# Two MoE stages behind a linear attention: the K^T V units placed in the first 32 steps, and the loads ahead of step 0 reordered

## The chip, the cores and the metric

One core of a Trainium2 chip runs the whole program. The metric is the device time of one execution in microseconds (us), the median of three runs. The profile and its trace come from one further execution.

## The reference

```
# q, k, v: (8, 8, 576, 64) float32; g_norm: (64)
kv  = einsum('bhsd,bhse->bhde', k, v)            # per batch and head, 64 x 64
out = einsum('bhsd,bhde->bhse', q, kv)
rms = sqrt(mean(out * out, axis=-1) + 1e-6)
x   = (out / rms * g_norm)                       # -> (4608, 512)
h   = x @ w_in                                   # (512, 2048)
g   = (a0 + a1 h + a2 h^2 + a3 h^3) / (1 + |b0||h| + |b1|h^2 + 1e-6)
x   = g @ w_out                                  # (2048, 512)
out = ((x @ w1) * (x @ w2)) @ w3 @ w_out2        # (512,1024), (512,1024), (1024,1024), (1024,512)
```

The weights reach the kernel as 64-bit floats.

## The kernel before, in words

**Prelude.** The order of work ahead of the first step is written out by hand as a string of letters. K loads the next K^T V unit, Q the next tile of 128 rows of q, W the next raw weight tile (512 KB), C converts a raw weight tile, F finishes pending conversions, c loads the constants and d works on them, k does a unit's matmuls (`kv_part`, `kv_out`), and t, o, r, n, x are the stages of a q tile: transpose, product with K^T V, root mean square, normalisation with a second transpose, and evacuation to the high and low parts `xh` and `xl`. All loads go through SP's one queue, in program order.

**Units.** K^T V of one batch is five units: four of 128 rows by 512 values of K and of V (256 KB each), and a short one of 64 rows (128 KB each). There are 8 batches and so 40 units, u = 0 to 39. A unit's 16 half-width matmuls on 64 columns add into the single PSUM tile `kv`; after the fifth unit of a batch `kv_out` copies the sum out, for batches 0 and 1 into `kvbd`, for later ones through a tile `kve` to memory (`kvd`), from which `kv_load` fetches it when its q tiles come up. K and V of a unit have two buffers each, `kt` and `vt`.

**Conversion.** A raw weight tile is made into float32 by one operation on ACT and three on DVE (L149, L151, L155, L159), and split into a high part on ACT (L84) and a low part on DVE (L85). A pending list holds back the split by up to two tiles. `wa0` to `wa15` are the 128-column slices of `w_in`, `wb0` to `wb15` the 128-row slices of `w_out`. There are 32 tiles; 11 are converted in the prelude and the others in steps 0 to 21, as many a step as the digits of `CONV` say.

**Steps.** 192 steps g follow, each one slice m of the hidden dimension for one block j of 384 rows. `l1(g)` is 12 matmuls into one of two PSUM tiles `h` (L88 to L90); ACT, POOL and DVE work on `h` in `ew1`, `ewy`, `ew2`, `ew3` (L536 to L573); `l2(g - 3)` is 12 matmuls into four tiles `acc` (L500 to L503). Within a step the string `MIX` sets the order in which pieces of these and of the conversions are issued. The first blocks go through the slices as block 0 with m = 0 to 7, block 1 with m = 0 to 15, block 0 with m = 8 to 15, and then block after block.

**What is hung onto the steps.** `todo` has, for a step and a place in it, further functions. Place 4 is the end of the step, behind `l2`, and place 0 its start. Units 8 to 39 are at the ends of steps 0, 1, 3, 5, ... 61, one a step; behind unit u's matmuls stands the load of unit u + 2, which waits until they have read the buffers. SP's queue is in order, so loads issued later wait behind that load. q tiles from 4 on have their stages in the steps too.

**After the steps** come the two later products, in 48 and 19 slots and a part between them; the change doesn't touch them.

Of the kernel before, what the change touches and what calls it, by code (L numbers as in the profile page):

```python
# [8 lines left out]
F32 = mybir.dt.float32  # L9
# [9 lines left out]
def linear_attention_two_moe_kernel(  # L19
# [25 lines left out]
    B, H, S, D = q.shape  # L45
# [3 lines left out]
    P = 128  # L49
    KD = DM // P  # L50
    NP = H // 2
    MF = DFF // P
# [12 lines left out]
    wp = ctx.enter_context(tc.tile_pool(name="wp", bufs=1))  # L65
# [28 lines left out]
    wa, wb = {}, {}  # L94
    bits = [t.bitcast(I32) for t in (w_in, w_out, w1, w2, w3, w_out2)]
    w_in_b, w_out_b, w1_b, w2_b, w3_b, w_out2_b = bits
    W = 512
# [39 lines left out]
    def mix(order, **gens):  # L137

        for c in order:
            next(gens[c], None)  # L140
        for gen in gens.values():
            run(gen)
# [79 lines left out]
    atp = atp_cm.__enter__()  # L222
# [3 lines left out]
    def segs(i):  # L226

        r, left = [], P
        t = i * P
        while left:  # L230
            b, s = divmod(t, S)
            n = min(left, S - s)
            r.append((P - left, n, b, s))
            t += n
            left -= n
        return r

    kt, vt, qt = {}, {}, {}

    def load_tok(i, src, d, tag):  # L240
        t = atp.tile([P, H, D], F32, tag=tag, name=tag, bufs=2)
        for r0, n, b, s in segs(i):
            nc.sync.dma_start(out=t[r0:r0 + n], in_=src[b, :, s:s + n, :].rearrange("h s d -> s h d"))
        d[i] = t

    MT = S // P
    NU = B * (NP + 1)
    HG = H // NP

    def load_kv(u):  # L250

        b, r = divmod(u, NP + 1)
        for src, d, tag in ((k, kt, "kt"), (v, vt, "vt")) if u < NU else ():
            t = atp.tile([P, H * D], F32, tag=tag, name=tag, bufs=2)
            if r < NP:
                nc.sync.dma_start(
                    out=t.rearrange("p (h f) -> p h f", h=HG),
                    in_=src[b, r * HG:(r + 1) * HG, 0:MT * P, :].rearrange("h (p t) d -> p h (t d)", t=MT),
                )
            else:  # L260
                nc.sync.dma_start(
                    out=t[0:S - MT * P].rearrange("p (h d) -> p h d", h=H),
                    in_=src[b, :, MT * P:, :].rearrange("h s d -> s h d"),
                )
            d[u] = t

    def load_q(i):
        if i < NTILE:
            load_tok(i, q, qt, "qt")
# [147 lines left out]
    with tc.manual_schedule():  # L417
# [36 lines left out]
        def k_next(u):  # L454
            kv_part(u)
            kv_out(u)

        tile_ops = {
            "K": (load_kv,), "Q": (load_q,), "k": (k_next,), "t": (q_pe, q_out), "o": (o_pe, n_sq),
            "r": (n_rms, n_rsq), "n": (n_out, x_pe), "x": (x_out,),  # L460
        }
        whole = {"W": w_load, "C": w_conv, "F": conv_flush, "c": consts, "d": const_ops}
        nc.vector.memset(unit, 1.0)
        nc.scalar.activation(out=unit, in_=unit, func=AF.Abs_reciprocal_sqrt)
        for op in "KQKWKcKdkQkCtWCWkCWCFkKWkWCCWCWQWtCQoCtoKWtKWKrrooWWKQknrrKnnxxkWnxWCQkCxW":
            if op in whole:
                whole[op]()
            else:
                i = count.get(op, 0)
                count[op] = i + 1  # L470
                for f in tile_ops[op]:
                    f(i)
# [105 lines left out]


        KV0 = 8  # L580
        KV_STEPS = [0, 1] + list(range(3, 4 * MF, 2))
        todo = {}

        def at_step(g, place, f, i):
            todo.setdefault((g, place), []).append((f, i))

        def do(g, place):
            for f, i in todo.get((g, place), ()):
                f(i)
# [3 lines left out]

        AT_G = [0, 5, 10]
        AT_W = [4, 7, 7, 10, 12, 13, 16, 18, 28, 30]
        for g, u in zip(KV_STEPS, range(KV0, NU)):
            at_step(g, 4, kv_part, u)
            at_step(g, 4, load_kv, u + 2)
            at_step(g + 1, 0, kv_out, u)
        at_step(2 * MF - 1, 4, kv_load, 2)  # L600
        for i in range(T0, NTILE):
            j, t = divmod(i, TPB)
            if j < 3:
                g = (-2 if j == 1 else 3 * HM - 3) + 3 * t
                when = ((q_pe, 0, 4), (q_next, 0, 4), (q_out, 1, 0), (o_pe, 1, 1), (n_sq, 1, 2), (n_rms, 1, 3),
                        (n_rsq, 1, 4), (n_out, 2, 0), (x_pe, 2, 4), (x_out, 3, 0))
            else:
                g = (j - 1) * MF + AT_G[t]
# [9 lines left out]
        for s in range(2 * KF2):  # L618
            src, c = (w1_b, w2_b)[s % 2].rearrange("(k p) f -> p k f", p=P), s // 2
# [490 lines left out]
                prod_d(f["a"], n, A12, B21, False, late)  # L1110
            e_load(n + 3)

        MIX = "nntltsuysltsttunuuu", "snsnalttaltyasnt", "ntsnnltlsyttst"
        CONV = "21011011120111111111110"
        NG = NBA * MF
        LB = NG - MF
# [117 lines left out]
        def u_some(n):  # L1234
            for i in range(n):
                if not next(chain, False):
                    break
                yield
# [19 lines left out]
        for j in range(NPR):  # L1258
# [8 lines left out]
            if j:  # L1267
                for c in range(5):
                    n = 5 * (j - 1) + c
# [19 lines left out]
        for g in range(NG + SK):  # L1289
# [28 lines left out]
            if LB < g:  # L1318
                gens["t"] = u_some(int(PREP[g - LB]))
            mix("".join(x for x in MIX[(g >= len(CONV)) + (g > LB)] if x in gens), **gens)  # L1320
            do(g, 2)
# [67 lines left out]
```

## Time and profile before

| | |
|---|---|
| median of three runs | 1559.38 us (1557.82 to 1559.94) |
| the profiled execution's own time | 1558.43 us |
| its span, from the first instruction to the last | 1556.7 us |
| TensorE matmul (PE) busy | 1515.8 us, 97% of the span |
| VectorE (DVE) busy | 1243.2 us, 80% |
| ScalarE (ACT) busy | 1056.5 us, 68% |
| GpSimd (POOL) busy | 225.0 us, 14% |
| share of PE in the chain that ended last | 85% |

The span is what the trace covers; 1.7 us of the execution's time lie around it. A busy share is a mean over stretches that differ: it tells where an engine is full only when it is read stretch by stretch. Step 0 begins at 47.12 us, step 8 at 94.55, step 21 at 161.53, step 32 at 218.61, step 48 at 298.43, step 64 at 377.68, step 80 at 450.43, step 96 at 523.18 and step 112 at 596.75: the stretches below are cut there.

### The profile page before, as it was taken

The numbers are of one execution on the slowest core, as the hardware profiler recorded it, in microseconds if no ns is written. First come the engines' busy times: TensorE is split into PE (matmuls) and PEld (weight loads), VectorE is DVE, ScalarE is ACT, GpSimd is POOL, SyncE is SP. The second block draws the span as 40 slices with busy tenths as digits, with TensorE's granted clock in tenths as the row PEclk, the third lists the DMA queues.
The fourth block names the chain that finished last, engine by engine and source line by source line (L and its number), as shares of the span: only waits on it lengthen the run. The fifth ranks groups of instructions, "written<-read, shape, count | busy, mean of one in ns | idle before, by whom it ended". The sixth has DMA issues, their size and how long they took to land.

```text
span 1556.7 us, 26099 instructions
## 1 busy us (share of the span) xinstructions
PE 1515.8 (97%) x9640; PEld 1477.4 (95%) x9640; DVE 1243.2 (80%) x2374; ACT 1056.5 (68%) x2109; POOL 225.0 (14%) x201
## 2 busy tenths in 40 slices
PE   4899999999999999999999999999999999999999
PEld 3788999999999999999999999999999999899999
DVE  5899968777889888988888889877677675688875
ACT  4688877787888888888888888544344343555554
POOL 0122221222222222222222221000000000000000
PEclk9799999999999999999999999999999999999999
DMA  9644243231112111110101021443543534434452
GB/s 281 194 141 140 72 112 99 82 96 45 48 38 69 42 45 42 45 55 28 58 28 56 6 69 37 146 146 112 190 141 117 190 119 164 140 110 154 155 160 89
DMA packets 153456, 157.95 MB, mean 101 GB/s; under 512 B 57328, under 2 KB 131312, under 8 KB 153328
## 3 DMA queue, kind: packets, MB, share of 16 engines
q1 hardware_dynamic: 153328, 156.28, 32.0%
q8 instruction: 76, 1.25, 0.3%
q14 instruction: 52, 0.43, 0.1%
HBM read 106.43 MB, written 49.81 MB: 100 GB/s over the span
## 4 chain that ended last, share of the span: by engine, by line
PE 85%; DVE 9%; ACT 3%; DMA 1%; issue 1%; POOL 1%; SPq 0%; DVEq 0%; POOLq 0%
PE acc L787 11%; PE h L88 8%; PE h L90 8%; PE h L89 8%; PE acc L500 7%; PE acc L501 7%; PE acc L503 7%; PE acc L1045 5%; PE h L787 5%; PE at L787 3%; PE kv L787 3%; PE h L1045 2%; PE kv L1045 2%; PE at L1045 2%; PE at L360 1%
## 5 line engine op out<-in xcount | busy, mean ns | idle before, releaser
L550 POOL TENSOR_TENSOR s<-z,a 128x384 f32<-128x384 f32 x192 | 223.3, 1163 | 732.6 <-ACT z L547 663.4
L553 DVE TENSOR_TENSOR n<-n,h 128x384 f32<-128x384 f32 x192 | 105.5, 550 | 91.9 <-ACT n L548 89.9
L546 ACT ACTIVATE a<-h 128x384 f32<-128x384 f32 x192 | 94.2, 491 | 98.3 <-PE h L90 97.6
L571 DVE SCALAR_TENSOR_TENSOR n<-n,na,y 128x384 f32<-128x384 f32 x192 | 155.4, 809 | 0.0
L562 ACT ACTIVATE y<-s,epsq 128x384 f32<-128x384 f32 x192 | 118.2, 616 | 44.7 <-POOL s L550 43.6
L547 ACT ACTIVATE z<-a,ab 128x384 f32<-128x384 f32 x192 | 136.2, 709 | 6.4
L548 ACT ACTIVATE n<-h,na 128x384 f32<-128x384 f32 x192 | 125.8, 655 | 0.0
L555 DVE SCALAR_TENSOR_TENSOR n<-n,na,h 128x384 f32<-128x384 f32 x192 | 116.4, 606 | 0.5
L569 DVE SCALAR_TENSOR_TENSOR s<-s,y 128x384 f32<-128x384 f32 x192 | 109.3, 569 | 0.0
L538 DVE TENSOR_TENSOR lo<-n,hi 128x384 fp32r<-128x384 f32 x192 | 106.9, 557 | 0.0
L573 DVE SCALAR_TENSOR_TENSOR n<-s,n 128x384 f32<-128x384 f32 x192 | 105.5, 550 | 0.2
L563 ACT ACTIVATE y<-y 128x384 f32<-128x384 f32 x192 | 101.0, 526 | 6.1
L536 ACT CAST hi<-n 128x384 fp32r<-128x384 f32 x192 | 96.1, 500 | 1.1 <-DVE n L573 1.1
L286 PEld LDWEIGHTS kv<-vt,kt 128*64 128x64 f32 (+1 forms) x640 | 24.7, 151 | 25.7 <-DMA kt<-in_k_dram 17.0
L286 PE MATMUL kv<-vt,kt 128*64 128x64 f32 (+1 forms) x640 | 30.4, 243 | 16.2 <-DMA vt<-in_v_dram 16.2
L829 ACT COPY p<-kv 128x384 f32<-128x384 f32 x24 | 11.5, 480 | 38.5 <-PE kv L787 26.9
L829 ACT COPY p<-acc 128x384 f32<-128x384 f32 x24 | 11.5, 480 | 38.5 <-PE acc L787 30.9
L844 ACT COPY u<-acc 128x384 f32<-128x384 f32 x24 | 11.5, 480 | 31.6 <-PE acc L787 31.6
L360 PE MATMUL at<-kvbd,qT 128*128 128x128 f32 (+1 forms) x216 | 29.2, 285 | 3.1 <-DVE kvbd L303 2.7
L360 PEld LDWEIGHTS at<-kvbd,qT 128*128 128x128 f32 (+1 forms) x216 | 26.6, 184 | 5.2 <-POOL s L550 3.0
L844 ACT COPY u<-h 128x384 f32<-128x384 f32 x24 | 11.5, 480 | 28.1 <-PE h L787 26.9
L379 DVE TENSOR_REDUCE ms<-sq 128x8 f32<-128x512 f32 x36 | 24.4, 683 | 5.9 <-ACT sq L373 5.9
(1440 smaller groups left out, 4923.0 us busy)
## 6 DMA issues: line engine op xcount, KB each, us to landing
ed<-eo SPq DMA_DIRECT2D x48, 384.0 KB, 2.6
er<-ed SPq DMA_DIRECT2D x35, 512.0 KB, 3.8
x2d<-xev SPq DMA_DIRECT2D x48, 192.0 KB, 2.0
xr<-x2d SPq DMA_DIRECT2D x48, 192.0 KB, 3.9
out_dram<-o SPq DMA_DIRECT2D x36, 256.0 KB, 2.0
kt<-in_k_dram SPq DMA_DIRECT2D x32, 256.0 KB, 2.8
vt<-in_v_dram SPq DMA_DIRECT2D x32, 256.0 KB, 3.2
qt<-in_q_dram SPq DMA_DIRECT2D x32, 256.0 KB, 3.1
```

The lines of the kernel that those rows point to most:

```text
L88: nc.tensor.matmul(outp, lhsT=lh, rhs=rh, start=first, stop=False)
L89: nc.tensor.matmul(outp, lhsT=lh, rhs=rl, start=False, stop=False)
L90: nc.tensor.matmul(outp, lhsT=ll, rhs=rh, start=False, stop=last)
L547: nc.scalar.activation(out=z, in_=a, func=AF.Identity, scale=ab[:, 1:2], bias=ab[:, 0:1])
L548: nc.scalar.activation(out=n, in_=h, func=AF.Identity, scale=na[:, 3:4], bias=na[:, 2:3])
L550: nc.gpsimd.tensor_tensor(out=s, in0=z, in1=a, op=ALU.mult)
L555: nc.vector.scalar_tensor_tensor(out=n, in0=n, scalar=na[:, 1:2], in1=h, op0=ALU.add, op1=ALU.mult)
L562: nc.scalar.activation(out=y, in_=e["s"], func=AF.Abs_reciprocal_sqrt, bias=epsq[:, 0:1])
L569: nc.vector.scalar_tensor_tensor(out=s, in0=s, scalar=EPS_Q, in1=y, op0=ALU.add, op1=ALU.mult)
L571: nc.vector.scalar_tensor_tensor(out=n, in0=n, scalar=na[:, 0:1], in1=y, op0=ALU.add, op1=ALU.mult)
L787: nc.tensor.matmul(bank, lhsT=lh[:, sl], rhs=x, start=first and kk == 0 and n == 0, stop=kk == 1 and n == 2, skip_group_check=True,)
L1045: nc.tensor.matmul(bank, lhsT=l[:, c, :], rhs=r, start=first and c == 0 and x == 0, stop=c == KH - 1 and x == 2, skip_group_check=True,)
```

## The change

The prelude's string is a new permutation of the same letters, with the same number of each. Units 0 to 9 are loaded into places of weight tiles that are needed late (`wb15` to `wb8`, `wa15`, `wa14`), K and V as the two halves of one place named `near`; q tiles 0 to 3 go two by two into `wa13` and `wa12`. So the first ten units have a place of their own each, and `kt` and `vt` begin with unit 10. `KVC` gives the number of units at the end of each of the steps 0 to 33; its 32 units end at step 30. Where two units stand at the end of one step, the first one's `kv_out` follows it at once. `MIX` has a new order in the steps with conversions (0 to 22).

```diff
+    late = [f"wb{i}" for i in range(MF - 1, MF // 2 - 1, -1)] + [f"wa{i}" for i in range(MF - 1, MF // 2 - 1, -1)]
+    NEAR = 2 * (NP + 1)
+
+    def in_slot(n):
+        return wp.tile([P, 2, W], F32, tag=late[n], name="near")
+
+    qnear = {}
+
     def load_tok(i, src, d, tag):
-        t = atp.tile([P, H, D], F32, tag=tag, name=tag, bufs=2)
+        if i < 4:
+            if i % 2 == 0:
+                qnear[i // 2] = in_slot(NEAR + i // 2)
+            t = qnear[i // 2][:, i % 2, :].rearrange("p (h d) -> p h d", h=H)
+        else:
+            t = atp.tile([P, H, D], F32, tag=tag, name=tag, bufs=2)
...
         b, r = divmod(u, NP + 1)
-        for src, d, tag in ((k, kt, "kt"), (v, vt, "vt")) if u < NU else ():
-            t = atp.tile([P, H * D], F32, tag=tag, name=tag, bufs=2)
+        if u < NEAR:
+            near = in_slot(u)
+        for n, (src, d, tag) in enumerate(((k, kt, "kt"), (v, vt, "vt")) if u < NU else ()):
+            t = near[:, n, :] if u < NEAR else atp.tile([P, H * D], F32, tag=tag, name=tag, bufs=2)
...
-        for op in "KQKWKcKdkQkCtWCWkCWCFkKWkWCCWCWQWtCQoCtoKWtKWKrrooWWKQknrrKnnxxkWnxWCQkCxW":
+        for op in "KKWCkWWCWFCCQcKKKWWtCCWQkWkQdWQkkCtKWCoKtCWooKtKrWrWoQKrknWWnrWnnxxxQCkCkx":
...
-        KV_STEPS = [0, 1] + list(range(3, 4 * MF, 2))
+        KVC = "1101012122011121212111110102101000"
+        KV_STEPS = [g for g, n in enumerate(KVC) for _ in range(int(n))]
...
-        for g, u in zip(KV_STEPS, range(KV0, NU)):
+        for n, (g, u) in enumerate(zip(KV_STEPS, range(KV0, NU))):
             at_step(g, 4, kv_part, u)
             at_step(g, 4, load_kv, u + 2)
-            at_step(g + 1, 0, kv_out, u)
+            at_step(*((g, 4) if KV_STEPS[n + 1:n + 2] == [g] else (g + 1, 0)), kv_out, u)
...
-        MIX = "nntltsuysltsttunuuu", "snsnalttaltyasnt", "ntsnnltlsyttst"
+        MIX = "nntlsutlsutstunuytu", "snsnalttaltyasnt", "ntsnnltlsyttst"
```

**At the start of SP's queue** the loads of units, q tiles, weights and constants stand in this order before:

```order
L256 DMA kt<-in_k_dram 128x2x256
L256 DMA vt<-in_v_dram 128x2x256
L243 DMA qt<-in_q_dram 128x8x64
L256 DMA kt<-in_k_dram 128x2x256
L256 DMA vt<-in_v_dram 128x2x256
L104 DMA wa0r<-in_moe_w_in_dram 128x4x256
L256 DMA kt<-in_k_dram 128x2x256
L256 DMA vt<-in_v_dram 128x2x256
L206 DMA co_a<-in_moe_a_dram 128x4
```

and in this order now:

```order
L271 DMA near<-in_k_dram 128x2x256
L271 DMA near<-in_v_dram 128x2x256
L271 DMA near<-in_k_dram 128x2x256
L271 DMA near<-in_v_dram 128x2x256
L104 DMA wa0r<-in_moe_w_in_dram 128x4x256
L104 DMA wa1r<-in_moe_w_in_dram 128x4x256
L104 DMA wa2r<-in_moe_w_in_dram 128x4x256
L104 DMA wa3r<-in_moe_w_in_dram 128x4x256
L256 DMA near<-in_q_dram 128x8x64
```

Four weight tiles moved ahead of the first q tile, of units 2 to 4 and of the constants; the next weight tile, `wb0r`, follows behind those in both orders.

**Ahead of step 0 on PE** stand the last units of the prelude and the transposes of the four normalised tiles `xt`, before:

```order
L286 MATMUL kv_363<-vt_305,kt_303 64x64 x8
L403 MATMUL acc1_376<-ident_75,xt_374 128x128 x4
L403 MATMUL acc2_401<-ident_75,xt_399 128x128 x4
L403 MATMUL acc3_410<-ident_75,xt_408 128x128 x4
L286 MATMUL kv_363<-vt_318,kt_316 64x64 x8
L403 MATMUL at_435<-ident_75,xt_433 128x128 x4
L286 MATMUL kv_363<-vt_324,kt_322 64x64 x8
L88 MATMUL h_482<-xh_415,wa0hl_186 128x384
```

and now:

```order
L301 MATMUL kv_361<-near_259 64x64 x8
L418 MATMUL acc1_374<-ident_75,xt_372 128x128 x4
L418 MATMUL acc2_387<-ident_75,xt_385 128x128 x4
L418 MATMUL acc3_404<-ident_75,xt_402 128x128 x4
L418 MATMUL at_413<-ident_75,xt_411 128x128 x4
L301 MATMUL kv_361<-near_279 64x64 x8
L301 MATMUL kv_361<-near_313 64x64 x8
L88 MATMUL h_470<-xh_418,wa0hl_132 128x384
```

One unit moved from ahead of the fourth transpose to behind it, so two units stand between that transpose and step 0.

**At the end of step 8 on PE**, between the last matmuls of `l2(5)` and the first of `l1(9)`, stands nothing before:

```order
L503 MATMUL acc0_697<-lo_960,wb5hl_772 128x384
L503 MATMUL acc1_698<-lo_960,wb5hl_772 128x384
L503 MATMUL acc2_699<-lo_960,wb5hl_772 128x384
L503 MATMUL acc3_700<-lo_960,wb5hl_772 128x384
L88 MATMUL h_1055<-xh_470,wa1hl_196 128x384
```

and now two units (15 and 16):

```order
L518 MATMUL acc0_685<-lo_972,wb5hl_757 128x384
L518 MATMUL acc1_686<-lo_972,wb5hl_757 128x384
L518 MATMUL acc2_687<-lo_972,wb5hl_757 128x384
L518 MATMUL acc3_688<-lo_972,wb5hl_757 128x384
L301 MATMUL kv_1070<-vt_936,kt_934 64x64 x8
L301 MATMUL kv_1070<-vt_1010,kt_1008 64x64 x8
L88 MATMUL h_1095<-xh_460,wa1hl_135 128x384
```

Counted over the whole program: steps 0 to 7 had 5 units and have 7 (one more at step 6, which had none and has two), steps 8 to 20 had 6 and have 17, steps 21 to 31 had 6 and have 8, steps 32 to 61 had 15 and have none.

## Rows read from the trace of the kernel before

**Rows 1.** Busy time by stretch: steps 0-7, 8-20, 21-31, 32-47, 48-63, 64-79, 96-111.
```profile
core 0: us, PE busy (x) PEld busy (x) DVE busy (x) ACT busy (x) POOL busy (x), PEclk, DMA share, GB/s
...
47.12:94.55 47.43, 42.23 (x279) 39.03 (x277) 40.73 (x80) 34.83 (x68) 9.55 (x8) 0.86 0.59 174
94.55:161.53 66.98, 62.14 (x409) 57.16 (x409) 66.95 (x132) 58.75 (x111) 20.28 (x14) 1.00 0.46 140
161.53:218.61 57.08, 56.81 (x408) 54.15 (x408) 49.10 (x95) 46.95 (x93) 13.17 (x12) 1.00 0.27 75
218.61:298.43 79.82, 79.54 (x564) 76.14 (x561) 61.23 (x125) 60.30 (x117) 16.61 (x16) 1.00 0.35 103
298.43:377.68 79.25, 79.25 (x556) 76.11 (x553) 60.51 (x123) 61.28 (x120) 16.47 (x17) 1.00 0.28 79
377.68:450.43 72.75, 72.75 (x434) 72.16 (x434) 63.78 (x124) 60.94 (x120) 18.25 (x17) 1.00 0.16 46
523.18:596.75 73.57, 73.57 (x442) 72.56 (x442) 63.79 (x124) 61.07 (x120) 18.28 (x17) 1.00 0.16 46
```

**Rows 2.** Timeline of PE (start, us): first matmuls of steps 44, 45 and 46.
```profile
279.57 0.42 PE L88 MATMUL h<-xh,wa12hl 128*128 128x384 f32 x1
...
283.86 0.34 PE L88 MATMUL h<-xh,wa13hl 128*128 128x384 f32 x1
...
288.77 0.44 PE L88 MATMUL h<-xh,wa14hl 128*128 128x384 f32 x1
```

**Rows 3.** The same, steps 17 and 18 (in brackets: idle before, and its releaser).
```profile
141.25 0.45 PE L88 MATMUL h<-xh,wa9hl 128*128 128x384 f32 x1 [0.60 <-DVE n L555]
...
146.32 0.44 PE L88 MATMUL h<-xh,wa10hl 128*128 128x384 f32 x1
```

**Rows 4.** PE's waits in steps 8 to 20: us in total, times, longest.
```profile
PE h L88 <- DVE n L555: 4.3, 7, 0.9
```

**Rows 5.** Timeline of DVE in the prelude: conversions, then the normalisation.
```profile
11.62 0.42 DVE L151 TENSOR_SCALAR wa0r<-wa0r 128x512 int32<-128x512 uint32 x1
...
25.37 0.43 DVE L151 TENSOR_SCALAR wb0r<-wb0r 128x512 int32<-128x512 uint32 x1
...
36.50 1.27 DVE L379 TENSOR_REDUCE ms<-sq 128x8 f32<-128x512 f32 x2
...
44.21 0.69 DVE L396 TENSOR_TENSOR xt<-acc,ny 128x512 f32<-128x512 f32 x1
```

**Rows 6.** Timeline of SP: the issue of the load of `wb0r`.
```profile
15.52 1.21 SPq L104 DMA_DIRECT2D wb0r<-in_moe_w_out_dram  x1
```

**Rows 7.** That load among the DMA issues: size, us from issue to landing.
```profile
wb0r<-in_moe_w_out_dram SPq DMA_DIRECT2D x1, 512.0 KB, 7.2
```

**Rows 8.** Timeline of PE: last transpose and unit of the prelude, step 0.
```profile
45.05 1.09 PE L403 MATMUL at<-ident,xt 128*128 128x128 f32 x4 [0.53 <-DVE xt L396]
46.06 1.12 PE L286 MATMUL kv<-vt,kt 128*64 128x64 f32 x16
47.12 0.69 PE L88 MATMUL h<-xh,wa0hl 128*128 128x384 f32 x1
...
50.07 0.34 PE L88 MATMUL h<-xh,wa0hl 128*128 128x384 f32 x1
```

**Rows 9.** Busy time by stretch, as rows 1: the prelude, and around step 0.
```profile
11.60:47.12 35.52, 17.99 (x151) 15.08 (x147) 30.15 (x58) 20.40 (x41) 0.00 (x0) 0.90 0.90 275
...
40.00:50.00 10.00, 8.20 (x53) 6.91 (x54) 9.18 (x21) 5.32 (x11) 0.00 (x0) 0.50 0.57 163
```

**Rows 10.** Timeline of SP: a unit's loads behind the unit of step 13.
```profile
126.08 0.38 SPq L256 DMA_DIRECT2D kt<-in_k_dram  x1
126.50 0.47 SPq L256 DMA_DIRECT2D vt<-in_v_dram  x1
```

**Rows 11.** The second of them among the DMA issues, as rows 7.
```profile
vt<-in_v_dram SPq DMA_DIRECT2D x1, 256.0 KB, 3.0
```

**Rows 12.** Timeline of PE: the wait of step 2.
```profile
64.70 1.94 PE L360 MATMUL at<-kvbd,qT 128*64 128x128 f32 x8 [2.75 <-DVE kvbd L303]
```

## The prediction

> **What bounds the kernel now.** The table has PE busy for 97% of the span, so I looked for stretches where a unit's matmuls cost nothing. Busy time by stretch [rows 1] shows three kinds. From step 32 on PE is full: 79.54 of 79.82 us, then 79.25 of 79.25, while DVE is busy for about 61. In steps 8 to 20 it is DVE that is full, 66.95 of 66.98 us, and PE has 66.98 - 62.14 = 4.84 us idle. In steps 0 to 7 PE has 47.43 - 42.23 = 5.2 us idle and DVE 6.7; they wait for each other. The waits [rows 4] name what PE waits for in steps 8 to 20: 4.3 us in 7 waits for DVE's L555, the last reader of a tile `h`. The timeline shows it in the small: step 18 has no unit, and step 17, which has one, begins after 0.60 us of idle time that follow step 16, which has none; yet step 17 takes 146.32 - 141.25 = 5.07 us [rows 3]. A unit is there paid out of idle time. Where PE is full it is not: step 44 without a unit takes 283.86 - 279.57 = 4.29 us and step 45 with one 288.77 - 283.86 = 4.91 [rows 2].
>
> Ahead of step 0 the engines are far from full: PE 17.99 of 35.52 us, DVE 30.15, and the DMA engines at 0.90 and 275 GB/s [rows 9]. DVE begins its first conversion at 11.62 and `wb0`'s at 25.37, and at 36.50 turns to the normalisation of the first four q tiles, which ends in step 0 at 47.12 [rows 5, 8].
>
> **The change part by part.**
>
> *Steps 32 to 63 lose 15 units.* The same 16 slices without units are there in the same trace: steps 64 to 79 in 72.75 us, and steps 96 to 111, which like 48 to 63 hold one q tile that spans two batches, in 73.57 [rows 1]. So steps 32 to 47 come down from 79.82 to 72.75 (7.07 us, 8 units) and steps 48 to 63 from 79.25 to 73.57 (5.68 us, 7 units): **-12.75 us**, or 0.85 a unit. The direct price of 0.62 [rows 2] would give 15 x 0.62 = 9.3; that is the small end. I take 12.75, since it compares whole stretches with the q stages in them.
>
> *Steps 21 to 31 gain 2 units.* PE is full but for 57.08 - 56.81 = 0.27 us [rows 1]. Two units at 0.62 to 0.88 are 1.2 to 1.8, less the idle time: **+1.3** (1.0 to 1.8).
>
> *Steps 8 to 20 gain 11 units,* 11 x 0.62 = 6.8 us of PE work, into 4.84 us of idle time. PE busy 62.14 + 6.8 = 68.96, against 66.98: **+2.0**. The small end is 0: DVE's own 66.95 us are a floor, and PE's, at 4.29 a step and 0.62 a unit, is 13 x 4.29 + 17 x 0.62 = 66.3. The large end is 6.8, if no idle time can be used. I take the sum of busy times, since PE needs 5.5 us in a step with two units and 4.9 in one with one, DVE 5.07 in either, and the two sorts alternate.
>
> *Steps 0 to 7 gain 2 units,* both at step 6, where PE has no idle time ahead of it worth counting; the 5.2 us lie mainly in the waits of steps 1 and 2, the longest of them 2.75 us for the copy of `kvbd` [rows 12]. **+1.3** (0 to 1.8). The new `MIX` keeps the same operations on DVE in a step, and where DVE is full their order doesn't change their sum: nothing. If a reordered operation came to wait, it would show as idle time of DVE, which has none in steps 8 to 20.
>
> *The prelude.* `wb0r`, issued at 15.52, landed 7.2 us later, at 22.7 [rows 6, 7]. Up to and with it 5.25 MiB are loaded before and 5.0 now, for one q tile went behind it: 256 KB at 275 GB/s is 0.95 us. SP also no longer waits, ahead of these loads, for the first units to leave `kt` and `vt`; that can be worth up to the missing tenth of the DMA engines' time, some 1 us. So `wb0r` lands at about 21.0. DVE, which has then been through `wa0` to `wa3`, begins `wb0` 25.37 - 21.0 = 4.4 us sooner. But low parts of two weights and the copy of `kvbd`, three operations of about 0.65 us (two reductions take 1.27 [rows 5]), and the small ones on the constants stand behind that place now and ahead of it before: 2.0 us. The normalisation begins 2.4 us sooner. Of its end: before, the fourth `xt` runs at 44.21, and its transpose and one unit at 45.05 and 46.06 bring step 0 to 47.12 [rows 5, 8]. Now two of the evacuations to `xl` (about 0.69 each) come behind that `xt` instead of ahead of it, -1.4, and a second unit stands on PE behind the transpose, +1.06. Step 0 comes 2.4 + 0.3 = **2.7 us sooner**. The ends are 0 (the loads of units 2 to 4, the q tile and the constants ahead of `wb0r` eat it up) and 4.7 (the held-back operations find room). The places borrowed from late weights cost nothing: their units and q tiles are through before those weights are loaded.
>
> Sum: -12.75 + 1.3 + 2.0 + 1.3 - 2.7 = -10.85 us. The profiled execution took 1558.43, so 1547.6; the median lies 0.95 above it: **1548.5 us**.
>
> **The rivals.**
>
> *The loads come late (slower).* Before, a unit's loads had three steps or more. Now 12 units (13, 14, 16, 17, 18, 23, 24, 26, 27, 29, 30, 38) are loaded behind the unit two ahead of them, and are needed one step later, after 4.29 + 0.62 = 4.9 us. The loads behind the unit of step 13 show what it takes in a quiet queue: K issued at 126.08, V at 126.50, V landed after 3.0 more, 3.4 in all [rows 10, 11]; 1.5 us to spare. Against that: in steps 6 to 9 the loads of units 14 to 20, five weight tiles and a q tile are 6.0 MB in some 20 us, 296 GB/s, as much as the DMA engines moved in the prelude at 0.90, and there a load took 7.2 us [rows 7, 9]. PE would stand at each such unit, with `l1` and `l2` of the next step behind it. The gain is gone when the 12 wait 10.85 / 12 = 0.9 us each, that is when V lands 5.8 us behind the unit; at 7.7 it is 12 x 2.8 = 33 us, 1582 us. For most steps the weights are 4 tiles ahead and the queue is near empty, which speaks for 3.4 to 4.5.
>
> *The idle time can't be used.* PE and DVE hand over twice a step with only two tiles `h`; after a double step PE is 0.5 us late, DVE might then wait, and the next step gives nothing back. Steps 8 to 20 then pay 6.8 and steps 0 to 7 1.8: 1548.5 + 4.8 + 0.5 = 1553.8. For it: DVE has no idle time to lend. Against: step 17 above.
>
> *The change moves cost and saves none.* If the 15 units cost in the first 32 steps the 0.85 that they cost later, only the start is left: 1559.38 - 2.7 = 1556.7.
>
> *Step 0 is no earlier:* 1551.2. For it: eleven loads, four of them small, now lie between those of `wa3r` and `wb0r`, and two before.
>
> *The clock.* From 40 to 50 us the granted clock was 0.50, that is 1.2 GHz, after a stretch in which PE worked for half of the time [rows 9]; nine matmuls of step 0 took 50.07 - 47.12 = 2.95 us [rows 8], against 9 x 4.29 / 24 = 1.61 at 2.4 GHz [rows 2]. A shorter prelude with the same matmuls in it might bring the higher clock to step 0 and one of steps 2 and 3: -2.7, 1545.8. The Trainium skill (TensorE: Matmul & The Clock Gate, Part 1: The HAM clock gate) says that the clock is held down by default and that activity releases it; by that rule a prelude with fewer gaps would run step 0 faster. The trace agrees that it was low after a sparse stretch; what it will be here no row shows, and the sum leaves it as it is.
>
> **How the numbers follow.** The forecast, with its terms moving within their bounds (1545.5 to 1551.5): 0.55. Step 0 no earlier, 1551.2: 0.13. Idle time not usable, 1553.8: 0.12. The clock, 1545.8: 0.10. No saving, 1556.7: 0.05. Loads late: 0.05, of which a fifth ends near the old time. The range 1543.5 to 1554 holds the first four nearly whole, somewhat over 8 in 10. A difference of 0.2% is 3.1 us, about what a measurement can tell. Faster by more: 0.55 + 0.13 + 0.12 + 0.10 = 0.90. Within: 0.05 + 0.01 = 0.06. Slower: 0.04.
>
> **What would show it.** Right: steps 32 to 63 in 146 to 147 us instead of 159.1, with no unit in them; PE's idle time in steps 8 to 20 near zero, DVE's a little above it, the stretch 67 to 70 us; step 0 at 44 to 45 us and DVE at `wb0` near 21. Wrong: in steps 7 to 20, waits of the unit's matmuls for the loads of K or V (none now); idle time of PE ahead of L88 left at 4 us with the stretch at 72 or more; step 0 still at 47; a granted clock of 0.50 in more than the stretch around steps 0 to 3.

## The result, and the profile after

The changed kernel takes 1546.27 us (median of 4, 1545.43 to 1547.06), the kernel before on the same chip 1558.92 (1557.82 to 1559.94): a ratio of 0.9919, 95% interval 0.9902 to 0.9936, 12.65 us faster. The profiled execution took 1547.06 us with a span of 1545.3, 11.4 less than before.

Busy time by stretch of the changed kernel, which answers to [rows 1]: steps 0-7, 8-20, 21-31, 32-47, 48-63, 64-79, with the same columns.

```profile
45.32:91.21 45.89, 41.07 (x310) 37.55 (x308) 42.17 (x83) 35.79 (x70) 9.28 (x8) 0.93 0.53 170
91.21:161.30 70.09, 67.77 (x588) 63.01 (x585) 66.80 (x131) 58.36 (x113) 16.31 (x13) 1.00 0.71 218
161.30:218.95 57.65, 57.65 (x444) 55.33 (x441) 46.80 (x93) 46.65 (x93) 11.61 (x11) 1.00 0.33 93
218.95:292.34 73.39, 73.10 (x434) 72.18 (x433) 63.98 (x125) 59.42 (x115) 17.33 (x17) 1.00 0.18 53
292.34:365.89 73.55, 73.55 (x441) 72.57 (x441) 63.80 (x124) 61.01 (x120) 18.24 (x17) 1.00 0.16 46
365.89:438.63 72.74, 72.74 (x433) 72.18 (x433) 63.80 (x124) 60.94 (x120) 18.25 (x17) 1.00 0.16 46
```

Steps 32 to 63 now read like 64 to 79. Against [rows 1], in us:

| term | forecast | measured |
|---|---|---|
| step 0 begins (47.12 to 45.32) | -2.7 | -1.80 |
| steps 0-7 | +1.3 | -1.54 |
| steps 8-20 | +2.0 | +3.11 |
| steps 21-31 | +1.3 | +0.57 |
| steps 32-63 | -12.75 | -12.13 |
| after step 63 | 0 | +0.4 |
| sum | -10.85 | -11.4 |

PE's waits in steps 0 to 31 of the changed kernel (us in total, times, longest), to be held against [rows 4, 12]:

```profile
PE h L88 <- DVE n L570: 2.3, 1, 2.3
PE at L375 <- DVE kvbd L318: 2.1, 1, 2.1
PE kv L301 <- DMA vt<-in_v_dram: 1.7, 2, 1.2
PE acc L515 <- ACT xev L540: 0.6, 1, 0.6
PE at L362 <- DVE xl L427: 0.2, 1, 0.2
PE at L375 <- ACT qT L367: 0.2, 1, 0.2
```

The many short waits for DVE's last reader of `h` (L555 before, L570 now) have gone from steps 8 to 20; the one left is in steps 0 to 2. The third row is new: two units waited for the load of V. The fourth is a wait for `xev`, the copy that ACT makes of a finished tile `acc`. The timeline of PE shows the longer wait for V, at the end of step 9 (units 15 and 16, then 17, then 18; between them `l1(9)` and `l2(6)`), and last the other, of unit 24 at the end of step 15:

```profile
95.61 1.43 PE L301 MATMUL kv<-vt,kt 128*64 128x64 f32 x32
96.97 0.44 PE L88 MATMUL h<-xh,wa1hl 128*128 128x384 f32 x1
...
101.37 0.69 PE L301 MATMUL kv<-vt,kt 128*64 128x64 f32 x16
103.22 0.69 PE L301 MATMUL kv<-vt,kt 128*64 128x64 f32 x16 [1.16 <-DMA vt<-in_v_dram]
103.84 0.44 PE L88 MATMUL h<-xh,wa2hl 128*128 128x384 f32 x1
...
150.68 0.68 PE L301 MATMUL kv<-vt,kt 64*64 64x64 f32 x16 [0.50 <-DMA vt<-in_v_dram]
```

SP issues the loads of units 17 and 18 behind units 15 and 16, and the last of the four took 5.2 us where [rows 11] had 3.0; first the timeline of SP, then that load among the DMA issues (size, us to landing):

```profile
96.34 0.38 SPq L271 DMA_DIRECT2D kt<-in_k_dram  x1
96.76 0.47 SPq L271 DMA_DIRECT2D vt<-in_v_dram  x1
97.33 0.41 SPq L271 DMA_DIRECT2D kt<-in_k_dram  x1
97.84 0.41 SPq L271 DMA_DIRECT2D vt<-in_v_dram  x1
```

```profile
vt<-in_v_dram SPq DMA_DIRECT2D x1, 256.0 KB, 5.2
```

V of unit 18 so landed at about 103.0, 6.1 us behind the end of unit 16.

**The prelude.** Timeline of DVE, which answers to [rows 5]:

```profile
22.33 0.43 DVE L151 TENSOR_SCALAR wb0r<-wb0r 128x512 int32<-128x512 uint32 x1 [5.01 <-DMA wb0r<-in_moe_w_out_dram]
...
35.58 1.86 DVE L394 TENSOR_REDUCE ms<-sq 128x8 f32<-128x512 f32 x3
...
41.62 0.69 DVE L411 TENSOR_TENSOR xt<-acc,ny 128x512 f32<-128x512 f32 x1
```

The load it waits for, as [rows 6, 7], on SP (behind the issue of the first of the constants) and then among the DMA issues:

```profile
6.77 3.04 SPq L206 DMA_DIRECT2D co_a<-in_moe_a_dram  x1
...
15.23 0.62 SPq L104 DMA_DIRECT2D wb0r<-in_moe_w_out_dram  x1
```

```profile
wb0r<-in_moe_w_out_dram SPq DMA_DIRECT2D x1, 512.0 KB, 7.1
```

PE behind it, as [rows 8]:

```profile
42.37 1.12 PE L418 MATMUL at<-ident,xt 128*128 128x128 f32 x4
43.41 1.98 PE L301 MATMUL kv<-near 128*64 128x64 f32 x32
45.32 0.44 PE L88 MATMUL h<-xh,wa0hl 128*128 128x384 f32 x1
...
47.00 0.34 PE L88 MATMUL h<-xh,wa0hl 128*128 128x384 f32 x1
```

Step 0 runs faster: nine matmuls in 47.00 - 45.32 = 1.68 us, against 2.95 in [rows 8]. Busy time in the prelude and from 40 to 50 us, as [rows 9], and in steps 0 and 2:

```profile
11.60:45.32 33.72, 19.75 (x176) 16.55 (x177) 26.70 (x53) 17.96 (x39) 0.00 (x0) 0.90 1.06 291
40.00:50.00 10.00, 9.36 (x82) 7.94 (x81) 9.45 (x21) 7.35 (x15) 0.96 (x1) 0.73 1.00 276
45.32:48.23 2.91, 2.91 (x31) 2.60 (x29) 2.74 (x6) 1.12 (x3) 0.00 (x0) 1.00 0.98 363
54.13:62.29 8.16, 5.91 (x28) 4.98 (x28) 8.10 (x15) 6.46 (x13) 2.74 (x2) 0.79 0.57 180
```

Steps 0 and 2 of the kernel before:

```profile
47.12:51.30 4.18, 4.18 (x30) 3.87 (x28) 3.90 (x8) 0.49 (x1) 0.00 (x0) 0.66 0.90 211
56.94:66.57 9.63, 6.77 (x28) 5.92 (x28) 9.53 (x18) 6.81 (x14) 3.25 (x2) 0.68 0.90 262
```

The granted clock rises from 0.66 to 1.00 in step 0 (-1.27 us) and from 0.68 to 0.79 in step 2 (-1.47 us, some of it a `kvbd` wait of 2.1 instead of 2.75). How much of this is the change's is open: the two later profiles of the changed kernel have 3.17 and 2.92 us in step 0 and 9.05 and 8.12 in step 2, and of the kernel before only one execution was profiled.

### The profile page after: what moved, and what is told of

Its sections match the earlier page's. It is cut to its first block, busy times and chain, and to the rows that moved or that the text cites. A ratio compares the mean times of both kernels' runs of the same rounds, so it can differ in the third digit from the quotient of the medians.

```text
span 1545.3 us, 26098 instructions
## 1 busy us (share of the span) xinstructions
PE 1508.2 (98%) x9640; PEld 1474.7 (95%) x9640; DVE 1247.8 (81%) x2374; ACT 1054.3 (68%) x2109; POOL 222.5 (14%) x201
## 4 chain that ended last, share of the span: by engine, by line
PE 89%; DVE 5%; DMA 2%; ACT 1%; issue 1%; SPq 1%; POOL 0%; DVEq 0%; POOLq 0%; ACTq 0%
PE acc L803 11%; PE h L88 9%; PE h L90 9%; PE h L89 9%; PE acc L515 8%; PE acc L516 8%; PE acc L518 8%; PE acc L1061 5%; PE h L803 5%; PE at L803 3%; PE kv L803 3%; PE h L1061 2%; PE kv L1061 2%; PE at L1061 2%; PE at L375 1%; DMA near<-in_q_dram 1%
## 5 line engine op out<-in xcount | busy, mean ns | idle before, releaser
L586 DVE SCALAR_TENSOR_TENSOR n<-n,na,y 128x384 f32<-128x384 f32 x192 | 162.2, 845 | 0.0
L570 DVE SCALAR_TENSOR_TENSOR n<-n,na,h 128x384 f32<-128x384 f32 x192 | 116.2, 605 | 0.5
L820 DVE TENSOR_TENSOR acc<-acc,u 128x384 f32<-128x384 f32 x24 | 13.6, 566 | 16.4 <-ACT u L860 16.1
L155 DVE SCALAR_TENSOR_TENSOR wb12r<-ct,wb12r 128x512 int32<-128x512 int32 x25 | 17.4, 694 | 10.0 <-ACT ct L149 9.4
```

Of the source, the lines that this page charges most:

```text
L586: nc.vector.scalar_tensor_tensor(out=n, in0=n, scalar=na[:, 0:1], in1=y, op0=ALU.add, op1=ALU.mult)
```

## The experiments

They ran in three groups, each on one chip with runs of the kernel before beside them: 1557.88 us in the first, 1559.54 in the second, 1559.39 in the third. The changed kernel ran again in the second and third. The theory at the outset: the gain is the units' move, paid partly out of idle time; the new string brings step 0 forward; places and `MIX` by themselves give nothing. The rivals: it is the start and the clock, or the units cost as much where they went.

**Units back where they were** (changed kernel, but):

```diff
-        KVC = "1101012122011121212111110102101000"
-        KV_STEPS = [g for g, n in enumerate(KVC) for _ in range(int(n))]
+        KV_STEPS = [0, 1] + list(range(3, 4 * MF, 2))
```

> The changed kernel with units 8 to 39 back at steps 0, 1, 3, 5, ... 61; the loads into the late places, the new string and the new MIX stay. My theory: the 15 units cost 0.81 us each where PE is full (12.1 us in steps 32 to 63) and about 3.7 us in steps 8 to 31, so this kernel is 8 to 9 us slower than the changed one: 1554 to 1556, and against the kernel before only the earlier start is left, 3 to 4.5 us. Rival (a unit costs the same wherever it stands): within 1.5 us of the changed kernel's 1546.3. Rival (the start gave nothing, the gain is all the units'): 1558 to 1559.

Measured: 1556.05 us, ratio 0.9987 (0.9978 to 0.9996), 1.8 us under the kernel before. Its stretch of steps 32 to 63:

```profile
215.71:374.72 159.01, 158.72 (x1116) 152.21 (x1113) 121.74 (x247) 121.55 (x237) 33.07 (x32) 1.00 0.31 91
```

Again 159.0 us, as before. Step 64 begins at 374.72, 8.8 us later than in the changed kernel, of the 11.8 that it gained there: most of the gain is the units'.

**The units' move alone** (kernel before, but):

```diff
-        KV_STEPS = [0, 1] + list(range(3, 4 * MF, 2))
+        KVC = "1101012122011121212111110102101000"
+        KV_STEPS = [g for g, n in enumerate(KVC) for _ in range(int(n))]
...
-            at_step(g + 1, 0, kv_out, u)
+            at_step(*((g, 4) if KV_STEPS[n + 1:n + 2] == [g] else (g + 1, 0)), kv_out, u)
```

> The kernel before with the new list of unit steps alone, each first unit of a pair followed at once by its copy out; string, buffers and MIX stay. My theory: 8 to 9 us faster than before, 1550 to 1551, if the two parts add; steps 32 to 63 at 147 us, steps 8 to 20 at 69 to 70 with one or two waits of a unit for its V. Rival (the units need the earlier start, since the loads of units 10 to 12 are behind the prelude's): 2 us less gain, 1552 to 1553, with waits in steps 3 to 8. Rival (a unit costs the same anywhere): no change, 1558 to 1559.

Measured: 1552.54 us (6 runs from 1548.92 to 1554.85), ratio 0.9963 (0.9950 to 0.9975). Steps 0-7, 8-20 and 32-63 of its profile, an execution of 1550.66 us:

```profile
46.87:95.87 49.00, 43.99 (x311) 40.45 (x309) 41.90 (x82) 35.27 (x68) 9.59 (x8) 0.86 0.60 177
95.87:164.70 68.83, 67.30 (x589) 62.85 (x585) 67.15 (x131) 58.54 (x113) 15.43 (x13) 1.00 0.74 221
222.42:369.37 146.95, 146.66 (x873) 144.71 (x873) 127.71 (x248) 120.49 (x234) 35.57 (x33) 1.00 0.17 49
```

At the same granted clock as before (0.86) steps 0 to 7 pay 49.00 - 47.43 = 1.57 for their two units, steps 8 to 20 1.85 for eleven, and steps 32 to 63 give back 12.12. In the profiles this run and the one above add up: step 64 comes 8.3 and 3.0 us sooner than before, together 11.3, and in the changed kernel 11.8. In the medians they don't (5.3 + 1.8 = 7.1, against 12.65); this run's six executions lie 5.9 us apart, and the difference is not settled. The median lies where the rival put it (the units need the earlier start, 1552 to 1553). That rival's waits in steps 3 to 8 are not in the profile, whose one wait for V, of 1.5 us, stands in step 9; but the profiled execution is 1.9 us under the median.

**The old `MIX`** (changed kernel, but):

```diff
-        MIX = "nntlsutlsutstunuytu", "snsnalttaltyasnt", "ntsnnltlsyttst"
+        MIX = "nntltsuysltsttunuuu", "snsnalttaltyasnt", "ntsnnltlsyttst"
```

> The changed kernel with the old MIX for the steps with conversions. My theory: DVE's sum in a step is the same, and PE, not DVE, is now the fuller in steps 8 to 20, so within 0.7 us of the changed kernel, 1545.5 to 1547. Rival (the new MIX is what shortened steps 0 to 7, by 1.5 us, and lets two units fit into a step): 1.5 to 4 us slower, 1548 to 1550, with waits of L88 for DVE's last reader of h in steps 8 to 20.

Measured: 1546.55 us, ratio 0.9929 (0.9917 to 0.9940): no difference from the changed kernel that can be measured. Steps 8 to 20 took 68.70 us and steps 0 to 7 took 47.82, in the slowest of its five executions (1548.29 us).

**The old string** (changed kernel, but):

```diff
-        for op in "KKWCkWWCWFCCQcKKKWWtCCWQkWkQdWQkkCtKWCoKtCWooKtKrWrWoQKrknWWnrWnnxxxQCkCkx":
+        for op in "KQKWKcKdkQkCtWCWkCWCFkKWkWCCWCWQWtCQoCtoKWtKWKrrooWWKQknrrKnnxxkWnxWCQkCxW":
```

> The changed kernel with the string of before; the loads into the late places, the units' new steps and the new MIX stay. My theory: the string brought step 0 forward by most of the 1.8 us measured, through the four weight tiles ahead; with the old one step 0 comes at 46.5 to 47.5 and the time is 1 to 2 us longer, 1547 to 1548.5. Rival (the places, which free SP from waiting for kt and vt, did it, and the string only reshuffles): step 0 at 45 to 45.8, 1546 to 1546.8. The clock can shift either by 1.3 us a step in steps 0 to 3; I read the start of step 0 and DVE's first conversion, not the time alone.

Measured: 1550.12 us, ratio 0.9948 (0.9936 to 0.9960), more than expected. The first matmul of step 0, at the lower clock:

```profile
47.60 0.69 PE L88 MATMUL h<-xh,wa0hl 128*128 128x384 f32 x1
```

The places alone don't bring step 0 forward; with them, the order of the loads does. The new order without the places was not run.

**The second group asks what still holds the changed kernel.** Three waits have rows: V in step 9, `kvbd` in step 2, `wb0` in the prelude. Either each costs what its row says, and taking it away gives that back; or what is won at one is lost at the next. The changed kernel beside them:

> The changed kernel once more, unchanged, as the reference on this chip for the three others: about 1546, and 0.992 of the kernel before.

Measured: 1546.03 us, ratio 0.9916 (0.9903 to 0.9930). Step 0 begins at 45.89 us and step 12 at 113.76; unit 18 waits 0.6 us for V in step 9.

Unit 18 at the end of step 10 instead of step 9:

```diff
-        KVC = "1101012122011121212111110102101000"
+        KVC = "1101012121111121212111110102101000"
```

> The changed kernel with unit 18 at step 10 instead of second at step 9. My theory: in the changed kernel unit 18 stood 1.16 us at the end of step 9, because its loads go out only behind unit 16 at the end of step 8, with unit 17's and two weight tiles beside them; with a step more the wait is gone and the time falls by 0.5 to 1.2 us. Rival (the queue itself is full there, whatever the lead): the wait moves to unit 18 in step 10 or to unit 19 in step 11, no change within 0.5 us.

Measured: 1545.90 us, ratio 0.9915 (0.9901 to 0.9929). PE's only wait from 91 to 115 us:

```profile
PE h L88 <- DVE n L570: 0.3, 1, 0.3
```

The V wait is gone, and step 12 begins at 113.65, 0.1 sooner: no difference.

Units 8 and 9 both at the end of step 0:

```diff
-        KVC = "1101012122011121212111110102101000"
+        KVC = "2001012122011121212111110102101000"
```

> The changed kernel with unit 9 behind unit 8 at the end of step 0, and none at the end of step 1. Unit 9 ends batch 1, so its copies to kvbd stand a step earlier on ACT and DVE. My theory: the 2.09 us in which PE waits in step 2 for DVE's copy of kvbd are idle time that nothing else needs, and they go: 1 to 2 us faster, steps 0 to 7 shorter by as much. Rival (DVE is the fuller engine in steps 0 to 4 and the copy only comes ahead of work that PE waits for next): the wait turns up ahead of L88 in steps 2 to 4, no change within 0.5 us. Rival (unit 9's loads haven't landed at the end of step 0): a wait of that unit for V in step 0, slower by up to 1 us.

Measured: 1545.28 us, ratio 0.9914 (0.9901 to 0.9928), 0.75 under the changed kernel and within the runs' spread. The `kvbd` wait is gone; two of PE's waits from 44 to 90 us stand for it:

```profile
PE h L88 <- DVE n L570: 4.6, 2, 2.8
PE at L362 <- DVE xl L427: 1.5, 1, 1.5
```

Step 8 begins at 90.00, 2.6 us sooner than in the run beside it, and step 12 at 112.98, 0.8 sooner. Some of the 2.6 is not the edit's: step 0, which the edit doesn't touch until its end, began at 44.77, 1.1 sooner.

`wb0`'s load and conversion ahead of the first q tile, the constants and the loads of units 2 to 4:

```diff
-        for op in "KKWCkWWCWFCCQcKKKWWtCCWQkWkQdWQkkCtKWCoKtCWooKtKrWrWoQKrknWWnrWnnxxxQCkCkx":
+        for op in "KKWCkWWCWFCCWCQcKKKWtCWQkWkQdWQkkCtKWCoKtCWooKtKrWrWoQKrknWWnrWnnxxxQCkCkx":
```

> The changed kernel with one W and one C of the string moved: wb0 is loaded and converted directly behind wa3, ahead of the first q tile, the constants and units 2 to 4. My theory: DVE's wait of 5.0 us for wb0 falls to under 3, DVE reaches the normalisation 1 to 2.4 us sooner, and so does step 0: 1 to 2 us faster, unless a lower clock in steps 0 to 3 takes it back. Rival (the DMA engines bound the prelude; what is loaded sooner puts the q tiles and units back): the wait moves to wa4 or to the first copy to kvbd, step 0 within 0.5 us of 45.3.

Measured: 1546.87 us, ratio 0.9916 (0.9903 to 0.9930): no difference. The next weight tile is late on DVE instead:

```profile
18.03 0.42 DVE L151 TENSOR_SCALAR wb0r<-wb0r 128x512 int32<-128x512 uint32 x1
...
24.14 0.43 DVE L151 TENSOR_SCALAR wa4r<-wa4r 128x512 int32<-128x512 uint32 x1 [3.56 <-DMA wa4r<-in_moe_w_in_dram]
```

Step 0 begins at 44.63, 1.3 sooner than in the run beside it, step 8 2.1 sooner, and step 12 at 113.52, 0.2 sooner. Where it went, PE's waits from 90 to 115 us:

```profile
PE kv L301 <- DMA vt<-in_v_dram: 1.1, 2, 0.8
PE acc L515 <- ACT xev L540: 1.0, 1, 1.0
```

One by one the three edits gave -0.1, -0.75 and +0.8 us: no wait is shown to be worth its row by itself.

**The third group** puts the three together: if the late V in step 9, and the wait for `xev` behind it, take what the start wins, then the three give together what none gives alone. It also asks why V is late, by the rival that the loads of units 17 and 18 are held up by the weight tiles loaded beside them. The changed kernel again:

> The changed kernel once more, unchanged, as the reference on this chip for the three others: about 1546.

Measured: 1547.63 us (6 runs from 1544.35 to 1548.71), ratio 0.9923 (0.9910 to 0.9935). Step 0 begins at 45.79 us and step 12 at 114.45; unit 18 waits 1.5 us for V in step 9.

All three edits (the string of the last edit, and):

```diff
-        KVC = "1101012122011121212111110102101000"
+        KVC = "2001012121111121212111110102101000"
```

> The changed kernel with all three edits tried singly: unit 9 behind unit 8 at step 0, unit 18 at step 10, wb0 loaded and converted behind wa3. Seen so far: whatever step 0 and steps 0 to 7 win, step 12 begins at 113.0 to 114.0 us in every variant, with a wait of unit 18 for its V in step 9 and one of l2's new acc for ACT's copies to xev in step 11. Theory A (the late V in step 9 holds it there): with that wait gone, the early start gets through, step 12 at 110 to 111.5, 2 to 3 us faster than the changed kernel. Theory B (ACT's four copies of acc in step 10 and the chain behind them hold it, as the wait of DVE for ACT at 113 suggests): step 12 at 112.5 to 113.5 and at most 1 us faster, with the wait for xev grown.

Measured: 1542.80 us (1542.25 to 1543.15), ratio 0.9895 (0.9882 to 0.9908): faster than both kernels, and 4.8 us under the changed kernel beside it, whose fastest run is 1544.35. Against the changed kernel's other two sets of runs (1546.03 and 1546.27) it is 3.2 and 3.5. The start of step 0; steps 8 to 20; and PE's waits from 86 to 115 us:

```profile
42.97 0.44 PE L88 MATMUL h<-xh,wa0hl 128*128 128x384 f32 x1
```

```profile
88.18:157.23 69.05, 67.74 (x588) 63.21 (x585) 66.82 (x132) 58.30 (x113) 16.11 (x13) 1.00 0.71 220
```

```profile
PE kv L301 <- DMA vt<-in_v_dram: 0.6, 1, 0.6
PE h L88 <- DVE n L570: 0.3, 1, 0.3
```

Step 0 is 2.8 us sooner than in the run beside it, and step 12 begins at 109.82, 4.6 sooner: what the start wins now comes through. The wait of 0.6 is unit 16's in step 8; none is left in step 9, and none of L515 for `xev`. But the start itself is earlier than the edit of the string alone made it. Up to step 0 this kernel and that one (step 0 at 44.63) have the same program, and of the 1.7 us between them 1.4 are there when DVE gets `wa4r`, at 22.74 instead of 24.14:

```profile
22.74 0.43 DVE L151 TENSOR_SCALAR wa4r<-wa4r 128x512 int32<-128x512 uint32 x1 [2.30 <-DMA wa4r<-in_moe_w_in_dram]
```

So part of the 4.6 us differs from execution to execution. From step 0 to step 12 this kernel takes 66.9 us, and the changed kernel's three profiles 67.9 to 68.7. Pairs of the three were not run, so which of them the third needs stays open.

A step's weight loads issued behind the loads of its units (changed kernel, but):

```diff
-                w_load(max(0, n_cv[0] + 4 - n_ld[0]))
...
             do(g, 4)
+            if g < len(CONV):
+                w_load(max(0, n_cv[0] + 4 - n_ld[0]))
```

> The changed kernel with the weight loads of steps 0 to 22 issued at the end of the step, behind the loads of units, instead of within it. Behind the loads of units 17 and 18 then stands one weight tile instead of two. Theory (the weight tiles beside it make unit 18's V late): the wait for V in step 9, 0.6 to 1.5 us in the changed kernel, falls to under 0.5; time 0.3 to 1 us less. Rival (two units' loads need that long by themselves, 4 x 256 KB behind SP's wait for unit 16): the wait stays at 0.6 or more. Rival: the weights now come late, waits of ACT and DVE for wa or wb tiles, 1 us or more slower.

Measured: 1548.64 us, ratio 0.9931 (0.9919 to 0.9943), no better. V of unit 18 is as long on its way (DMA issues), and PE waits for V as before, from 91 to 115 us:

```profile
vt<-in_v_dram SPq DMA_DIRECT2D x1, 256.0 KB, 5.5
```

```profile
PE kv L301 <- DMA vt<-in_v_dram: 1.8, 2, 1.1
```

So issuing the weights behind them doesn't bring V sooner. What makes it late stays open, since in this run too weight tiles lie around the four loads of units 17 and 18. The tile of the step before, issued at 92.29, landed at 98.3, after the first of the four had been issued at 96.38, and the next was issued at 98.64, 0.5 us behind V:

```profile
wa12r<-in_moe_w_in_dram SPq DMA_DIRECT2D x1, 512.0 KB, 6.0
```

With the order unchanged the last of the four took 5.2, 4.4 and 5.5 us in the changed kernel's three profiles. No run has the four loads alone.

That order of loads with the three edits:

> All three edits and the weight loads at the end of the step. If theory A for the first kernel of this call holds and the weights are not late, as it or up to 0.5 us faster; if the weights come late, slower than it by 1 us or more.

Measured: 1543.35 us, ratio 0.9898 (0.9883 to 0.9912), as without it (1542.80). A third buffer for `kt` and `vt` was not tried.

## Why the prediction was right

The time fell 2.2 us under the forecast and inside the range. Most of the 2.2 lies between the profiled execution and the median: the forecast added 0.95 us for that, and the median came out 0.79 under the profiled execution. The terms themselves missed by 0.55 (-11.4 for -10.85). The main step held: 15 units out of steps 32 to 63, priced by equal stretches without them, gave 12.13 of 12.75 us. The missing 0.6 is partly a wait of 0.29 in steps 32 to 47, which was there before (79.82 - 79.54 = 0.28) and which steps 64 to 79 don't have. The direct price of 0.62 a unit (9.3) would have been too little. Four smaller terms were off, by up to 2.8 us, and nearly cancelled; that is luck. The time also lies within 0.5 us of the clock rival's 1545.8.

- *Steps 8 to 20, +3.11 for +2.0.* The eleven units took 3.11 us there (1.85 when they moved alone) instead of the 6.8 that "idle not usable" gave them, so the idle time could be used, and "saves none" falls with the 12.1 us that steps 32 to 63 gave back. PE's busy time came out lower than summed (67.77 for 68.96), at 0.51 us a unit. What went wrong is the loads, which the sum put at nothing: the prediction took 3.4 us, one unit's loads in a quiet queue, where two units' loads stand one behind the other. V landed 6.1 us behind the unit, past the 4.9 there were. The rival "loads late" was true for 2 of its 12 units: 1.7 us of waits, and 0.6 for `xev` with them, which are the stretch's idle time (70.09 - 67.77 = 2.32).
- *Steps 0 to 7, -1.54 for +1.3.* The price of the two units was right: step 6 went from 4.66 to 5.89 us, +1.23, and the units' move alone paid 1.57. But steps 0 and 2 lost 2.74 us, as the clock rival had it (-2.7). It came on top of the forecast, which left the clock as it was. That the change brought all of it is not shown, since executions of one kernel differ as much as 1.2 us in these two steps. Not all of it lasts either: the changed kernel's three profiles have steps 0 to 7 at 45.89, 46.70 and 45.91 us and steps 8 to 20 at 70.09, 68.49 and 70.48.
- *The start, -1.80 for -2.7.* The step that failed is the landing of `wb0r` at 21.0: it landed at 22.3, since the eleven loads between `wa3r` and it kept SP busy until 15.23, 0.3 us before the old time. The issue of `co_a` alone took 3.04 us there, and 0.47 before; the forecast counted bytes and took no time for issuing. DVE waited 5.0 us for `wb0r`, began it 3.0 sooner instead of 4.4, and the held-back operations took 2.1 of that (2.0 forecast). The end of the prelude gave 0.9 instead of 0.3.
- *Steps 21 to 31, +0.57 for +1.3:* the two units used the 0.27 us of idle time and cost less than the direct price.
- *`MIX`, nothing:* right as far as the time shows, which putting the old order back did not change; DVE is busy 66.80 of 70.09 us.

By its own signs the forecast was right in steps 32 to 63 (146.94 us, where it had 146 to 147). It just missed in steps 8 to 20 (70.09, where it had 67 to 70), and it missed in the start of step 0 (45.32, where it had 44 to 45) and in DVE's reaching `wb0` (22.33, where it had 21). One sign of being wrong appeared, the waits for V.

From 38.5 to 45.3 us PE worked for 6.10 of 6.80 us at a granted clock of 0.50, and then step 0 ran at 1.00. The Trainium skill (TensorE: Matmul & The Clock Gate, Part 1: The HAM clock gate) has the clock held down until activity releases it. The trace agrees as far as that. That a fuller prelude is what did it is not shown: PE was busy for 19.75 of 33.72 us in this profile and for 18.33 of 34.19 in the third of the changed kernel, both with step 0 at 1.00, and for 19.93 of 33.66 with the units back, with step 0 at 0.83.

## What to carry to other kernels

Move work out of stretches where its engine is full into stretches where it waits, and price the gain by an equal stretch without that work, not by the work's own duration. Where two loads' consumers come closer together, take the landing time of the pair, one behind the other, not that of one load: the last of four took 4.4 to 5.5 us here, with weight tiles around them, and one in a quiet queue 3.0. An early gain can be lost at the next wait downstream: three edits that gave at most 0.75 us one by one gave 3.2 to 4.8 together.

## What the runs showed of the hardware

The kernel before doesn't always get the same clock. In the first group its 17 runs fall into nine with a mean granted clock of 0.995 to 0.998 (1556.24 to 1557.88 us) and eight with 0.993 (1558.35 to 1561.08). In the other two groups the times overlap: 1557.94 us stands at 0.993 and 1559.40 at 0.995. The units' move alone has its fastest run, 1548.92, at 0.996 and its slowest, 1554.85, at 0.992. The changed kernel's times don't go by it: in the second group 1545.69 us stand at 0.991 and 1546.46 at 0.996, which fits with early gains being given back in steps 8 to 11, but doesn't show it.
